# The opening of a recurrence-and-MLP kernel's written order of work, permuted

## The chip, the cores and the metric

The kernel runs on one core of a Trainium2 chip. A core has a matrix engine (TensorE, PE), which loads 64 x 64 weights into its array (PEld) and streams matmuls through it, and three engines for elementwise work: VectorE (DVE), ScalarE (ACT) and GpSimd (POOL). SyncE (SP) only issues DMAs here. Each engine has its own list of instructions and works through it in order; an instruction that has to wait for another engine or for a DMA holds up all that stands behind it on its own engine. Matmuls write to PSUM, from which DVE and ACT read.

The metric is the device time of one execution in microseconds (us). It has to be as low as it can get.

## The reference

Two blocks follow each other. The first is a recurrence over 768 tokens for 4 batches and 8 heads, each with a 40 x 40 state (all in float32):

```python
for t in range(S):
    kt, vt, rt = (k[:, :, t], v[:, :, t], r[:, :, t])
    wt, at, bt = (w[:, :, t], a[:, :, t], b[:, :, t])
    y[:, :, t] = np.einsum('bhd,bhde->bhe', rt, state)
    Sa = np.einsum('bhde,bhe->bhd', state, at)
    state_decay = state * wt[:, :, None, :] - np.einsum('bhd,bhe->bhde', Sa, bt)
    state = state_decay + np.einsum('bhd,bhe->bhde', vt, kt)
```

The second takes `y`, with the 8 heads of a token put side by side to 320 numbers, as 3072 tokens through an MLP with a quick GELU:

```python
h = x @ w_in                               # 320 -> 2048
g = h * (1.0 / (1.0 + np.exp(-1.702 * h)))
return (g @ w_out).astype(np.float32)      # 2048 -> 320
```

## The kernel before, in words

**Tiles and stages.** The sequence is cut into 12 chunks of 64 tokens and the 4 batches into 2 pairs, which gives 24 units; unit i is chunk i // 2 for pair i % 2. Within a unit the 64 steps are not done one by one: the products of the decays are built as exponentials of running sums of their logarithms, the coupling of the 64 tokens through `a` and `b` becomes a triangular 64 x 64 matrix for each head, and this matrix is inverted in five doubling levels. So a unit depends on the unit two places ahead of it (same batches, chunk before) through its state alone. Each unit goes through these steps, by the names of the functions:

- `load_w`, `load`: DMAs of logw and wc (the decay), ak, b, rv, RV (v) and time, all on SP.
- `logarithm` and `decay`: ACT takes the logarithm; PE forms running sums (`by_time` into ps_cum, `by_channel` into ps_cumc); ACT takes exponentials, FT, GT and wch (`exp_of_product`, L565 and L569) and G (`exp_by_time`, L591).
- `prep`: DVE or POOL multiplies ak, b and time by these; PE forms A (`score_A`) and RV (`score_RV`).
- `inverse`: PE forms N (`score_N`), then come five levels. For units 0 to 3 (`plain_level`) a level is 32 + 8 matmuls into ps_level, a copy PT of the pair on ACT (L784) and a transpose EX of the same pair on DVE (L723); the next level needs both. After level 4 come a transpose ES and its spread T (L702, L707), four copies Tc (L797), two half-size products, ps_Q (`off_one`) and ps_T21 (`off_two`), and the finished T on DVE (L830).
- `solve`: from unit 2 on, the state of unit i − 2 is turned and read (ps_zT, ps_rz). The known parts (ps_B0, ps_B1), then ps_X = T times B on PE, M on DVE (L907), then ps_y, whose parts are the new state and the unit's outputs. x, the outputs times FT (`decayed`, L953, on DVE or POOL), goes to DRAM (`part_with`) and comes back transposed as xT (`get_back`).
- `mlp(c)` after every second unit: for q = 0 to 3 ten up matmul groups (`up`, ps_up) and a GELU on ACT, then two down products of eight parts (`down`, ps_down) and a store.

**Weights.** The MLP's weights come as 64-bit words, in 8 weights of 4 DMAs each, and are rebuilt as floats during the opening: `rebased` on ACT (L447), `bounded`, `shifted` and `rounded` on DVE (L451, L455, L459, 128 x 1280 elements each), `joined` on POOL (L463). Weights 0 to 3 are those of up, 4 to 7 those of down; a down product needs all of 4 to 7 part by part.

**The order.** `Plan.add` collects 2700 tasks with their dependencies, numbered in the order of the calls. No scheduler runs at build time: the string `ORDER` is the whole schedule. `Plan.listed` (L89) reads it, and L1046 runs it through:

```python
tasks = plan.listed(ORDER)
for t in tasks:
    t.fn(t)
```

A token such as `209p1` is the number of a task, the engine that does it (p PE, a ACT, d DVE, g POOL, s SP) and, where the task uses PSUM, which of the four pairs of banks it takes. Each engine's instructions come in the order in which their tokens stand. Where two engines read one pair, they do so in turn, in the list's order. A string is allowed if every task stands behind those it depends on, and if the engine is one that the task offers.

SP's DMAs use eight semaphores in turn; in the trace a DMA is issued only once the one eight places ahead of it has landed.

These task numbers come up in the lists:

| task | unit 0 | unit 1 | unit 2 | unit 3 |
|---|---|---|---|---|
| cum, cumc (PE) | 87, 88 | 142, 143 | 264, 265 | 334, 335 |
| A, N (PE) | 98, 103 | 154, 159 | 283, 288 | 353, 358 |
| levels 0 to 4 (PE) | 107, 110, 113, 116, 119 | 163, 166, 169, 172, 175 | 292, 295, 298, 301, 304 | 362, 365, 368, 371, 374 |
| Q, X, y (PE) | 126, 134, 136 | 182, 190, 192 | 311, 326, 328 | 381, 396, 398 |
| x to DRAM, xT back (SP) | 140, 141 | 196, 197 | 332, 333 | 402, 403 |

470 is cum of unit 4; 198 to 207, 209 to 218, 220 to 229 and 231 to 240 are the first MLP's up tasks, 242 to 249 and 253 to 260 its down tasks. Weight 0's DMAs are 15 to 18, and each further weight's are nine numbers on (24 to 27, 33 to 36, up to 78 to 81); the five tasks that rebuild it follow its DMAs.

Of the kernel before, what the change touches and what calls it, by code (L numbers as in the profile page):

```python
# [58 lines left out]
class Plan:  # L59
# [29 lines left out]
    def listed(self, text):  # L89

        assert len(text.split()) == len(self.tasks)
        table, out, done = "exp", [], set()
        for one in text.split():
            e = next(e for e in ENGINES if ENGINES[e] in one)
            n, bank = one.split(ENGINES[e])
            t = self.tasks[int(n)]
            assert e in t.engines and t.after <= done and (e == "SP" or (t.pair is None) == (not bank))
            t.engine, t.bank = e, int(bank or 0)
            if e == "ACT" and t.table:
                t.load, table = t.table != table, t.table  # L100
            done.add(t)
            out.append(t)
        return out
# [4 lines left out]
0s 8s 26s 5s 7s 9s 3a 6s 87p0 88p1 24s 89a1 1s 2s 12s 102a 95d 100p2 90a0 93d 158a 101d2 98p3 96g 10s 94d 17s 97g 16s 99d3  # L108
103p1 4a 11s 132p0 104a1 105d1 142p2 143p3 133a0 106d 130p1 14s 144a3 13s 107p0 15s 18s 151g 108a0 109d0 51s 131a1 110p3 27s
149g 150d 111a3 112d3 159p0 156p1 145a2 161d0 160a0 152g 113p3 345s 92a 162d 25s 153d 114a3 163p2 42s 115d3 34s 19a 274s 264p0  # L110
165d2 265p3 164a2 22d 266a3 166p2 20d 273s 21d 33s 43s 167a2 154p3 168d2 23g 35s 28a 157d1 116p2 155d3 169p1 117a2 118d2 267a0
279d 63s 280g 119p3 277s 171d1 36s 44s 123a3 120d3 343s 125d3 121a 278g 124d3 29d 287a 126p2 170a1 288p0 127a2 30d 172p1 479s
122a3 31d 289a0 128p2 54s 173a1 45s 129d2 32g 62s 174d1 134p3 37a 290d0 175p2 344s 135d3 180a2 146s 178a2 275s 176d2 136p1
179a2 38d 181a2 39d 177a 282g 276s 291d 91s 138a1 182p0 188p3 281d 183a0 186p2 139d 137a1 283p0 187a2 184p1 189a3 40d 140s
292p2 46a 60s 284d0 41g 285p3 185d1 148a 286d3 190p0 293a2 294d2 334p1 335p3 357a 191d0 141s 268g 147s 336a3 315d 192p2 47d
337a1 348d 316p0 194a2 346s 295p3 349d 61s 317a0 195g 347s 358p1 296a3 297d3 360d1 318a0 298p3 271a 361d 319p0 338g 300d3 196s
193a2 320a0 355p2 385d 270s 48d 299a3 362p0 356d2 351g 301p3 363a0 364d0 350g 386p2 197s 302d3 365p0 387a2 269s 352g 359a1
303d3 388a2 323p1 367d0 366a0 321p3 49d 324a1 304p2 322a3 478s 325d1 50g 353p0 309a2 470p3 354d0 209p1 307a2 210p1 310a2 305d2
211p1 308a2 272d 198p0 341a 199p0 72s 212p1 70s 64a 200p0 340s 368p2 52s 342d 339s 69s 201p0 369a2 202p0 370d2 203p0 471a
213p1 65d 214p1 389p2 66d 472a3 483g 204p0 390a2 560s 371p3 67d 306a 53s 215p1 71s 482s 216p1 372a3 217p1 476a 220p2 373d3 68g  # L120
218p1 221p2 477d 219a1 205p0 222p2 206p0 223p2 224p2 78s 559s 207p0 55a 311p3 225p2 79s 312d3 80s 226p2 208a0 58d 313p1 374p3
314d1 227p2 56d 379a3 228p2 229p2 57d 326p0 230a2 59g 393p1 327d0 378a3 391p2 394a1 375d3 231p0 558s 392d2 376a 232p0 233p0
395d1 81s 73a 234p0 480s 381p2 235p0 474s 328p1 475s 382a2 74d 377a3 485d 380a3 236p0 75d 481s 492a 242p2 486d 243p2 82a 76d
484d 77g 383p3 237p0 384d3 244p2 329d1 330d1 488p3 473d 238p0 531d 245p2 487g 246p2 489d3 85d 532p1 708s 239p0 533a1 396p3
331d 534a1 240p0 247p2 397d3 332s 241a0 562s 535p1 83d 490p3 536a1 84d 398p0 706s 572a 491d3 86g 550p1 253p3 399d0 551a 555s
400d0 561s 333s 254p3 401d 255p3 552a1 564d 493p0 402s 556a 567g 570p1 554s 494d0 248p2 705s 563d 566g 249p2 495d0 498d 256p3
571d1 565g 403s 250a2 496a0 251d2 696p1 497g 557d 539p0 252s 537p2 257p3 538a2 704s 540d0 701s 258p3 553d 611d 697a 499d 573p2
259p3 576a2 574d2 784s 710d 700s 260p3 787s 541d0 575d2 404p0 578d 261a3 577g 405p0 579d 698a1 568p2 711g 500p1 406p0 569d2
501a1 407p0 262d3 580p2 702a 502d1 263s 408p0 582d2 409p0 503d 410p0 583d 504a 612p3 411p0 584g 613d3 412p0 614d3 413p0 505p1
709d 414a0 426p3 506d1 427p3 428p3 507d1 429p3 699d 581d2 430p3 615p1 703d 431p3 616a1 785s 585p0 432p3 508d 586a0 433p3 587d0  # L130
434p3 509a 588d 435p3 589d 448p2 436a3 510p1 590p0 511a1 449p2 592d0 591a0 512d1 415p3 513d 416p3 593d 514a 417p3 594g 418p3
515p0 419p3 516a0 517d0 595p1 518d 420p3 596a1 597d1 421p3 598d 422p3 519a 599d 423p3 424p3 520p0 425a3 437p1 521d0 438p1
523d0 522g 439p1 524d0 440p1 525d0 441p1 442p1 526d0 527p3 718p0 528a3 443p1 719d0 929s 444p1 720d0 529p3 445p1 721d0 446p1
530d3 600p0 723d 447a1 542p3 722d 724g 603d0 605a0 619p1 604d0 543d3 450p2 620a1 606d0 544p3 621d1 601d0 602d 617p1 707s 546d3
451p2 618a1 783s 712d 547g 713d 607p0 725p1 608a0 452p2 609p0 453p2 548s 610d0 932s 454p2 727d1 726d1 622p0 728d 545d3 729a
775p1 455p2 623d0 780s 776a 549s 756d 730p3 624p0 456d2 457d2 731d3 458s 459p2 777a1 778g 732d3 786s 788g 781a 779s 626d0
460p2 625d0 627g 733d 795p1 835d 734a 461p2 735p3 791g 462p2 628s 736a3 796d1 737d3 716p0 792g 738d 463p2 782d 739g 1011s
920p1 757p3 925s 464p2 717d0 758a3 629s 759a3 790d 465p2 740p0 789d 466p2 741a0 742d0 921a 797p3 467d2 760p0 1008s 468d2 800a3
923d 652p2 469s 761d0 922a1 653p2 926a 930s 798d3 714p1 799d3 654p2 924s 802d 801g 655p2 934d 803a 656p2 836p0 657p2 715d1
658p2 659p2 837d0 762p3 838d0 927d 660p2 763a3 661p2 764p1 662a2 743d 630p0 744d 928s 631p0 632p0 765d1 804p3 766d1 633p0  # L140
805a3 806d3 634p0 807d 635p0 808a 745p2 636p0 748d2 637p0 749d2 839p1 933g 750d2 638p0 840a1 1009s 751d2 639p0 809p3 746d2
935g 640a0 641p1 810d3 642p1 793p2 747a 811d3 674p0 812d 794d2 813a 752p3 643p1 753a3 814p2 644p1 815a2 816d2 754p3 645p1
755d3 646p1 817d 647p1 818a 767p2 841p3 768d2 648p1 842a3 649p1 819p2 650p1 820a2 821d2 769p3 822d 651a1 823d 675p0 771d3 931s
770d3 772g 824p2 936d 676p0 827a2 828a2 942p1 829a2 677p0 1153s 830a2 937d 945a1 773s 663p3 825d2 664p3 943d1 1156s 826a 665p3
944d1 999p2 947d 946g 666p3 1000a 1004s 980d 940p1 948g 667p3 941d1 668p3 774s 669p3 670p3 831p1 671p3 1001a2 1002d 1003s
832d1 672p3 1005a 1013d 678p0 673a3 1006d 833p2 843p1 679p0 834d2 1007s 844d1 938p2 845d1 680p0 939d2 846p3 681p0 847d3 949p1
# [983 lines left out]
```

## Time and profile before

| what | value |
|---|---|
| time, median of 3 runs | 678.8 us (678.29 to 679.48) |
| profiled execution, its own time | 682.79 us |
| span in the trace, first to last instruction | 681.1 us |
| mean granted TensorE clock | 0.990 |
| DMA bytes moved | 69.73 MB, mean 102 GB/s |

The profiled execution is one of its own and took 4.0 us more than the median of the three timed runs; sums that are made from its rows are made against 682.79, not against 678.8.

How to read it: busy times are summed over an engine's instructions. A digit in the line of slices is the busy share of one fortieth of the span, 17 us, in tenths. PEclk is the granted clock of TensorE on the same scale, where 9 is 90% or more. In tables by stretches, each engine has its busy time, with the number of instructions in brackets, then come the mean granted clock as a share of full speed, the busy share of the DMA engines and the bytes moved in a second. In lists of waits, a row names the waiting engine and line, behind the arrow what released it, then the total in us, how often, and the longest. In the timeline a row has the start and the duration, then engine, line, operation, result and operand; in square brackets stands the engine's idle time just before it, with what ended it.

### The profile page before, as it was taken

Reading aid. Unit: us, or ns where it says so; the run is one execution under the profiler, and the core shown is the slowest. Engines: PE = TensorE matmul, PEld = TensorE weight load, DVE = VectorE, ACT = ScalarE, POOL = GpSimd, SP = SyncE. Lnnn points to the kernel's source line nnn. Section 1 sums busy time; section 2 is a strip of 40 time slices with the busy share of each in tenths; the row PEclk is TensorE's granted clock in tenths of the full one; section 3 lists DMA queues with packets and bytes.
Section 4 is the critical chain, followed back from the end, with each engine's and each line's share of the span. In section 5 each row is a group of like instructions: output and inputs, shape, how many; then the busy total and the mean of one; then the engine's idle time right before and its main releaser. Section 6 shows DMA issues by size and latency. Waiting matters only on the chain.

```text
span 681.1 us, 42181 instructions
## 1 busy us (share of the span) xinstructions
PE 652.0 (96%) x19488; PEld 572.4 (84%) x19488; DVE 445.5 (65%) x906; ACT 330.7 (49%) x688; POOL 176.7 (26%) x204
## 2 busy tenths in 40 slices
PE   5777999999999999999999999999999999999997
PEld 5667888997987788888888898899899799889996
DVE  4687877777867668767776587868556766675001
ACT  4675845544564654664545445455454354252110
POOL 5443444225123123123123211321412421300000
PEclk9788999999999999999999999999999999999999
DMA  7874755205314314432404413513502312200100
GB/s 235 275 244 148 228 158 173 89 14 155 108 50 139 103 45 125 124 108 67 121 23 131 140 34 107 154 33 106 149 29 71 121 51 58 58 13 23 51 12 21
DMA packets 35312, 69.73 MB, mean 102 GB/s; under 512 B 5440, under 2 KB 14656, under 8 KB 35136
## 3 DMA queue, kind: packets, MB, share of 16 engines
q1 hardware_dynamic: 35136, 67.03, 32.8%
q8 instruction: 153, 2.51, 1.6%
q14 instruction: 23, 0.19, 0.1%
HBM read 59.15 MB, written 7.86 MB: 98 GB/s over the span
## 4 chain that ended last, share of the span: by engine, by line
PE 91%; DMA 4%; ACT 1%; DVE 1%; issue 1%; SPq 0%; ACTq 0%; DVEq 0%
PE ps_up L300 31%; PE ps_down L300 30%; PE ps_level L300 9%; PE ps_y L300 5%; PE ps_B L300 4%; PE ps_X L300 2%; PE ps_N L300 2%; PE ps_rz L300 2%; PE ps_RV L300 2%; PE ps_A L300 1%; DMA ak<-in_ak 1%; PE ps_zT L300 1%; PE ps_Q L300 1%; DMA time<-in_time 1%; PE ps_T L300 1%
## 5 line engine op out<-in xcount | busy, mean ns | idle before, releaser
L300 PE MATMUL ps_up<-xT_all,w_sb 64*64 64x256 f32 x3840 | 254.4, 377 | 2.0 <-DMA xT_all<-x_dram 1.1
L300 PE MATMUL ps_down<-w_sb,g 64*64 64x320 f32 x3072 | 240.3, 430 | 1.1 <-issue 0.9
L300 PEld LDWEIGHTS ps_up<-xT_all,w_sb 64*64 64x64 f32 x3840 | 172.9, 133 | 17.7 <-issue 2.5
L300 PEld LDWEIGHTS ps_down<-w_sb,g 64*64 64x64 f32 x3072 | 143.3, 133 | 31.4 <-issue 1.6
L988 ACT ACTIVATE g<-ps_up 128x1024 f32<-128x1024 f32 x48 | 49.1, 1024 | 44.7 <-PE ps_up L300 44.3
L709 POOL TENSOR_TENSOR EX<-ES,quads 128x512 f32<-128x512 f32 x29 | 38.3, 1323 | 115.5 <-DVE ES L702 83.1
L751 ACT COPY W<-ps_level 128x512 f32<-128x512 f32 x56 | 32.7, 585 | 69.1 <-PE ps_level L300 67.4
L300 PEld LDWEIGHTS ps_level<-W,EX 64*64 64x64 f32 x2560 | 59.2, 134 | 5.8 <-DVE T L830 0.2
L300 PE MATMUL ps_level<-W,EX 64*64 64x64 f32 (+1 forms) x2560 | 56.2, 217 | 0.0
L753 DVE TENSOR_TENSOR E<-two,ps_level 128x256 f32<-128x256 f32 x80 | 33.1, 415 | 34.7 <-ACT W L751 30.7
L707 ACT ACTIVATE EX<-ES,quads 128x256 f32<-128x256 f32 x80 | 36.3, 501 | 30.4 <-DVE ES L702 29.9
L619 POOL TENSOR_TENSOR ak<-ak,FT 128x512 f32<-128x512 f32 x16 | 22.0, 1378 | 76.2 <-DMA ak<-in_ak 54.4
L300 PE MATMUL ps_level<-PT,EX 64*64 64x64 f32 (+2 forms) x1280 | 34.9, 244 | 5.7 <-DVE EX L723 4.8
L300 PEld LDWEIGHTS ps_level<-PT,EX 64*64 64x64 f32 x1280 | 32.6, 145 | 8.9 <-DVE EX L723 5.7
L702 DVE STREAM_TRANSPOSE ES<-E 128x256 f32<-128x256 f32 x80 | 35.2, 442 | 4.7 <-DVE E L753 0.5
L300 PE MATMUL ps_y<-M,bh 64*64 64x104 f32 (+1 forms) x768 | 34.8, 247 | 1.3 <-DVE M L907 0.8
L300 PE MATMUL ps_y<-RV,kh 64*64 64x104 f32 (+1 forms) x768 | 34.9, 247 | 0.3 <-DVE EX L723 0.3
L891 ACT COPY B<-ps_B 128x416 f32<-128x416 f32 (+1 forms) x34 | 16.5, 492 | 33.5 <-PE ps_B L300 33.2
L300 PEld LDWEIGHTS ps_y<-RV,kh 64*64 64x64 f32 x768 | 28.9, 133 | 2.0 <-DVE M L907 0.5
L907 DVE TENSOR_TENSOR M<-ps_X,later 128x832 f32<-128x832 f32 (+1 forms) x24 | 23.8, 993 | 9.8 <-PE ps_X L300 9.5
L627 POOL TENSOR_TENSOR kh<-time,G 128x320 f32<-128x320 f32 x18 | 16.2, 902 | 48.4 <-PE ps_y L300 34.4
L300 PEld LDWEIGHTS ps_y<-M,bh 64*64 64x64 f32 x768 | 27.0, 133 | 1.9 <-DVE M L907 1.2
(131 smaller groups left out, 1097.2 us busy)
## 6 DMA issues: line engine op xcount, KB each, us to landing
ak<-in_ak SPq DMA_DIRECT2D x48, 160.0 KB
rv<-in_rv SPq DMA_DIRECT2D x48, 160.0 KB
time<-in_time SPq DMA_DIRECT2D x24, 320.0 KB
xT_all<-x_dram SPq DMA_DIRECT2D x48, 160.0 KB
wc<-in_wc SPq DMA_DIRECT2D x20, 264.0 KB
logw<-in_w SPq DMA_DIRECT2D x24, 160.0 KB
RV<-in_v SPq DMA_DIRECT2D x24, 160.0 KB
b<-in_b SPq DMA_DIRECT2D x48, 80.0 KB
```

The costliest lines, as they stand in the source:

```text
L300: nc.tensor.matmul(o, lhsT, rhs, start=start, stop=True, skip_group_check=True)
L619: plan.add(R, {"DVE": 690.0, "POOL": 1270.0, "sbuf": True}, lambda t: of(t.engine).tensor_mul(ahT(), ahT(), FT_of(i)), reads=T("ak", "FT") ...
L627: plan.add(R + 4, {"POOL": 870.0, "DVE": 490.0, "sbuf": True}, lambda t, n=n, dst=dst: of(t.engine).tensor_mul(dst(i)[:, :, :D], by_head(t ...
L702: plan.add(rank, dve(256), lambda t: nc.vector.transpose(ES(n), source(t)), writes=[key("ES", n, 6)], **reads)
L707: nc.scalar.activation(dst[:, :, h], ES(n), ACT.Copy, scale=quads[:, h, :1])
L709: of(t.engine).tensor_mul(dst, ES(n).unsqueeze(2).to_broadcast([128, 8, 2, 32]), quads.unsqueeze(1).to_broadcast([128, 8, 2, 32]))
L751: plan.add(rank, any2(512), lambda t: copy(t.engine)(tiles_of(W(n + 1)), blocks(psum(t, ""), 64)), writes=[key("W", n + 1, 5)], pair=pair)
L753: plan.add(rank, dve(256), lambda t: nc.vector.tensor_sub(tiles_of(E(n + 1)), every(two32, [128, 2, 4, 32]), blocks(psum(t, ""), 64)[:, :, ...
L891: plan.add(R, any2(4 * wide), lambda t: copy(t.engine)(dst(), some(psum(t, "")[:, :, :208])), writes=[("Bv", i)] if x and c > 0 else T("B" ...
L907: plan.add(R + 1, dve(8 * wide), lambda t: nc.vector.tensor_tensor(M_of(i)[:, :, :wide].rearrange("p (j b) n -> p b j n", b=2), some(psum( ...
L988: plan.add(-45, {"ACT": 1030.0, "table": "gelu"}, lambda t: nc.scalar.activation(g_of(c * NQ + q).rearrange("p m r n -> p r m n"), psum(t, ...
```

## The change

The change has two parts. In `Plan.listed` an SP token may carry a digit, which is stored in a field `window` of the task; no token of the new list has one on SP, and nothing reads the field. And the string `ORDER` is replaced. The new string holds the same 2700 tasks. It differs from the old one in its opening: from PE's 155th task on (of 1080, task 430), ACT's 103rd, DVE's 144th, POOL's 27th and SP's 94th (of 268), each engine's tasks come in the order that they had before. 43 tasks have another engine: DVE has 795 of them (785 before), ACT 427 (433) and POOL 130 (134). The numbers of the PSUM pairs are dealt out anew.

The opening of both lists, to a little beyond the first MLP's first up:

```diff
@@ Plan.listed
             t.engine, t.bank = e, int(bank or 0)
+            if e == "SP":
+                t.window = t.bank
             if e == "ACT" and t.table:
...
 ORDER = """
-0s 8s 26s 5s 7s 9s 3a 6s 87p0 88p1 24s 89a1 1s 2s 12s 102a 95d 100p2 90a0 93d 158a 101d2 98p3 96g 10s 94d 17s 97g 16s 99d3
-103p1 4a 11s 132p0 104a1 105d1 142p2 143p3 133a0 106d 130p1 14s 144a3 13s 107p0 15s 18s 151g 108a0 109d0 51s 131a1 110p3 27s
-149g 150d 111a3 112d3 159p0 156p1 145a2 161d0 160a0 152g 113p3 345s 92a 162d 25s 153d 114a3 163p2 42s 115d3 34s 19a 274s 264p0
-165d2 265p3 164a2 22d 266a3 166p2 20d 273s 21d 33s 43s 167a2 154p3 168d2 23g 35s 28a 157d1 116p2 155d3 169p1 117a2 118d2 267a0
-279d 63s 280g 119p3 277s 171d1 36s 44s 123a3 120d3 343s 125d3 121a 278g 124d3 29d 287a 126p2 170a1 288p0 127a2 30d 172p1 479s
-122a3 31d 289a0 128p2 54s 173a1 45s 129d2 32g 62s 174d1 134p3 37a 290d0 175p2 344s 135d3 180a2 146s 178a2 275s 176d2 136p1
-179a2 38d 181a2 39d 177a 282g 276s 291d 91s 138a1 182p0 188p3 281d 183a0 186p2 139d 137a1 283p0 187a2 184p1 189a3 40d 140s
-292p2 46a 60s 284d0 41g 285p3 185d1 148a 286d3 190p0 293a2 294d2 334p1 335p3 357a 191d0 141s 268g 147s 336a3 315d 192p2 47d
-337a1 348d 316p0 194a2 346s 295p3 349d 61s 317a0 195g 347s 358p1 296a3 297d3 360d1 318a0 298p3 271a 361d 319p0 338g 300d3 196s
-193a2 320a0 355p2 385d 270s 48d 299a3 362p0 356d2 351g 301p3 363a0 364d0 350g 386p2 197s 302d3 365p0 387a2 269s 352g 359a1
-303d3 388a2 323p1 367d0 366a0 321p3 49d 324a1 304p2 322a3 478s 325d1 50g 353p0 309a2 470p3 354d0 209p1 307a2 210p1 310a2 305d2
-211p1 308a2 272d 198p0 341a 199p0 72s 212p1 70s 64a 200p0 340s 368p2 52s 342d 339s 69s 201p0 369a2 202p0 370d2 203p0 471a
...
+0s 2s 7s 8s 5s 9s 3a 6s 87p0 88p1 1s 26s 100p2 13s 89a1 146s 15s 90a0 93d 95d 101d2 98p3 12s 96d 10s 94d 4a 92a 33s 99d3 102a
+14s 97d 130p1 103p0 132p2 11s 105d0 143p3 106d 133a2 131a1 16s 142p2 104d0 17s 107p1 144a3 24s 51s 18s 108a1 149d 145a2 109d1
+158a 110p0 153g 150d 112d0 159p3 111d0 156p2 161d3 113p1 345s 157d2 277s 151d 25s 27s 114a1 162d 35s 274s 152d 19a 163p0 115d1
+52s 265p2 164a0 22d 116p1 160a3 273s 165d0 20d 166p3 43s 21d 264p0 266a2 118d1 23g 168d3 28a 117d1 154p2 155d2 119p1 267a0
+167a3 279d 63s 34s 29d 45s 169p0 123a1 60s 278g 36s 120d1 344s 171d0 121a 270s 268g 30d 91s 280g 287a 126p2 170a0 288p3 127d2
+125a1 289d3 172p2 343s 290d3 122a1 124a1 31d 44s 173a2 128p0 32g 129d0 174d2 134p3 37a 275s 175p1 135d3 178a1 38d 136p0 148a
+179a1 39d 181a1 291d 188p2 137a0 282g 276s 186p3 176d1 42s 138a0 180d1 281g 177a 283p0 139d 189a2 182p1 292p2 183a1 40d 140s
+187a3 147s 357a 184p1 284d0 41g 285p3 293a2 185d1 334p0 46a 286d3 190p1 141s 294d2 335p3 269s 191d1 295p2 336a3 47d 192p1
+337a0 315d 296a2 349d 355p3 346s 194a1 316p0 348d 347s 193a1 195g 338d 297d2 317a0 358p1 318a0 298p2 360d1 361d 359a1 319p0
+196s 299a2 385d 362p1 352g 341a 300d2 350g 364d1 301p2 320a0 356d3 197s 363a1 386p0 303d2 323p3 340s 387a0 388a0 49d 321p1
+302a2 365p0 324d3 478s 325d3 62s 304p2 48d 366a0 61s 198p3 339s 322a1 199p3 50g 367d0 200p3 271a 310d2 368p1 305d2 307d2 209p0
+369d1 210p0 308a2 211p0 309a2 69s 212p0 351d 70s 201p3 370d1 71s 202p3 479s 272d 389p2 470p1 203p3 390a2 213p0 306d 471a 214p0
+342d 353p2 204p3 472a1 485g 474s 205p3 72s 476a 371p1 354d2 53s 482s 64a 480s 206p3 477d 215p0 473g 54s 216p0 492a 220p2 221p2
...
```

## The prediction

> **What bounds the kernel now.** I read the page's busy times and slices first. TensorE (PE) is busy 96% of the span, and only the first slices and the last have idle time.
>
> ```profile
> PE 652.0 (96%) x19488; PEld 572.4 (84%) x19488; DVE 445.5 (65%) x906; ACT 330.7 (49%) x688; POOL 176.7 (26%) x204
> PE   5777999999999999999999999999999999999997
> PEclk9788999999999999999999999999999999999999
> ```
>
> The change permutes the opening alone and PE's list is the same from its 155th task on, so its worth is PE's idle time in the first 70 us (four slices of 17 us). A table by stretches shows where (columns: stretch, its length, busy us of PE, weight load, DVE, ACT and POOL, clock, DMA share, GB/s).
>
> ```profile
> 0.00:26.00 26.00, 16.31 (x436) 15.02 (x440) 12.39 (x21) 11.46 (x32) 13.27 (x45) 0.87 0.79 243
> 26.00:48.00 22.00, 14.98 (x596) 13.15 (x592) 18.26 (x33) 16.59 (x44) 9.74 (x5) 0.92 0.88 280
> 48.00:58.00 10.00, 7.23 (x312) 6.37 (x304) 7.15 (x12) 7.22 (x19) 5.00 (x7) 1.00 0.65 199
> 58.00:69.00 11.00, 9.82 (x400) 9.34 (x396) 8.26 (x12) 5.99 (x14) 4.89 (x4) 0.84 0.31 86
> 69.00:95.00 26.00, 25.32 (x673) 22.05 (x666) 21.76 (x28) 21.39 (x44) 9.37 (x5) 1.00 0.73 230
> ```
>
> Between 26 and 69 PE idles 43.0 − 32.0 = 11.0 us; after 69, where the MLP's first up matmul starts (69.0), hardly at all. So the question is at what time PE reaches that up with its other work done, and whether it can run on. The waits up to 70 us name what it waits for.
>
> ```profile
> DVE EX L723 <- ACT PT L784: 11.7, 8, 3.2
> PE ps_level L300 <- DVE EX L723: 4.8, 5, 1.7
> PE ps_Q L300 <- ACT T L707: 3.2, 2, 2.0
> ```
>
> These are the inversion of units 0 and 1: level on PE, copy PT on ACT, transpose EX on DVE, next level. The transpose reads the same PSUM pair as the copy and starts when the copy ends. The timeline shows that list order, too, costs time.
>
> ```profile
> 25.41 1.50 DVE L723 STREAM_TRANSPOSE EX<-ps_level 128x512 f32<-128x512 f32 x2 [1.63 <-ACT PT L784]
> ...
> 29.18 0.69 PE L300 MATMUL ps_A<-ak 40*64 40x64 f32 x32 [0.28 <-ACT wch L569]
> ...
> 30.63 0.89 PE L300 MATMUL ps_level<-PT,EX 64*64 64x96 f32 x32 [0.76 <-DVE EX L723]
> ```
>
> The two transposes at 25.41 belong to units 0 (level 2) and 1 (level 0). Unit 0's was done at 26.13, but its level 3 began at 30.63, because PE's list has cum and cumc of unit 2, unit 1's level 1 and unit 1's A (waiting for ACT's exponentials) before it.
>
> Last, the clock, in windows of 3.41 us.
>
> ```profile
> 15.72:19.14 3.42, 1.73 (x63) 1.31 (x61) 0.72 (x1) 1.78 (x8) 1.86 (x2) 1.00 0.86 297
> 19.14:22.55 3.41, 2.82 (x90) 2.45 (x86) 1.99 (x3) 1.14 (x2) 1.50 (x2) 0.50 0.90 316
> 32.79:36.20 3.41, 0.92 (x40) 0.67 (x40) 3.24 (x8) 1.44 (x6) 2.44 (x2) 1.00 0.93 287
> 36.20:39.62 3.42, 3.34 (x100) 3.35 (x104) 2.43 (x4) 2.18 (x8) 0.84 (x1) 0.50 0.80 288
> 56.68:60.10 3.42, 1.49 (x64) 1.35 (x68) 3.08 (x6) 2.12 (x5) 0.41 (x1) 1.00 0.59 196
> 60.10:63.51 3.41, 3.41 (x108) 3.38 (x100) 2.03 (x2) 1.48 (x3) 3.28 (x3) 0.50 0.62 178
> ```
>
> Half clock follows a window with at most 1.73 us of PE work, never one with 2.13 or more. A half-clock window costs up to 1.7 us of PE work.
>
> **The change, part by part.** It removes and adds no instruction: 2700 tasks before and after. The added line stores a field that nothing reads. What moves is order, the engine of 43 tasks, and pair numbers. I follow the two dependency chains through the new lists with durations from before's rows, and DMA landings from before's, shifted by the bytes ahead of each at 243 to 280 GB/s.
>
> *SP.* logw of unit 1 moves behind logw of unit 0 and a piece of weight 0 goes ahead of unit 1's rv and ak: I get ak(0) 7.8 us (6.72 before), logw(1) 10.3 (11.49), ak(1) 17.1 (15.83), b(1) 19.5 (18.14). With eight DMAs in the air an issue follows a landing (5.79 after 5.78), so these slips add. Weight 0's last piece slips from 21.41 to about 25.0, and the last of weight 3 to about 40.3 from 37.69; late weights hold up ACT, which rebases them in list order. Unit 1's level 0 ends up at 24.5 against 24.11: nothing gained up to there.
>
> *PE and ACT, 26 to 48.* Unit 0's level 3 is now listed ahead of unit 2's sums: from 30.63 to 26.5. Level 4 goes from 33.41 only to 31.95, because DVE and ACT take other work between. Unit 0's Q goes from 36.28 to 35.4, its X from 40.56 to 39.05, its state from 42.72 to 40.85. Unit 1's level 2 gets later (31.56 to 33.45: unit 2's exponentials and weight 1 stand ahead of its copy on ACT), its level 3 earlier (37.61 to 36.65), and its Q not at all (45.53 to 45.55: ACT, in order, waits for that late weight piece). Gain here: 1.7 us on unit 0, 0 on unit 1.
>
> *26 to 40, clock.* The new list leaves PE some 1.55 us of work in 29.4 to 32.8, under 1.73, so I take half clock from 32.8 to 39.6. It costs unit 0 0.9 us (X at 39.95); unit 1 waits for the weight anyway. Ends: 0 and 0.9; I take 0.9, which changes nothing in the sum below, since unit 1 ends it.
>
> *48 to 69.* Unit 1's X comes at 48.3 (49.54), its y ends at 52.3 (53.96). Unit 2's levels now stand before unit 1's work, not behind it: its level 2 at 54.2 (57.76), its rz at 55.3 (58.69). From about 49.7 PE has no stall over 0.5 us, where before it idled 2.8 us in 48 to 58 and 1.2 in 58 to 69, and ran at half clock from 60.10 to 63.51; with PE full from 50 on that window goes. PE reaches the first up at 62.5 instead of 69.01: 6.5 us earlier. Before, its list has A of unit 3 (0.70) and cum of unit 4 (0.45) ahead of it, now behind: 6.5 − 1.15 = **5.35 us**. The up's input xT of unit 1 lands at about 60.6 (62.45), 1.9 us before it is needed.
>
> *DVE and POOL.* DVE gets 10 tasks more (18.4 us in 26.5 to 45.8, 95%; before 18.26 of 22, 83%). A weight's tensor_scalar takes 0.82 us alone and 1.53 at 44.43, beside a POOL operation: +0.7. Of 12 in before's first 69 us two met one. In the new lists I find two more, in the stretch where unit 1 has no slack (1.4 us); ends: none (0) and all twelve (8.4). I take 1.4, by the one or two met in before. 5.35 − 1.4 = **4.0 us**.
>
> *After 69.* PE now reaches the first down at 90.0 (93.53). Its weight, joined by POOL, comes at 89.0 (89.56). It fits by 1.0. Then the lists agree and PE, busy 97%, keeps the lead.
>
> The profiled execution took 682.79 (span 681.1), 4.0 above the median of 678.8, so it becomes 678.8, and the median 678.8 − 4.0 = **674.8**. Differences of up to 0.2% (1.4 us) can hardly be told from no change.
>
> **The clock, by trace and by rule.** Before 19.14, 36.20 and 60.10 the clock halved after windows in which PE was busy 1.73, 0.92 and 1.49 us of 3.41, its longest gaps being 1.25 to 1.95 us. The Trainium skill's "TensorE: Matmul & The Clock Gate" ("Part 1: The HAM clock gate" and "Why this matters for your kernels") lets the half clock come back only after at least one idle window, and asks to avoid gaps over some 3 us. By that rule nothing in the changed kernel would go cold and the 0.9 us above would be saved; the trace disagrees three times, so I keep its pattern.
>
> **The rivals.**
> - *More half clock.* The new list moves idle time about, and two more windows may fall to 1.73 or less, in 39 to 50. Each costs up to 1.7 us: 674.8 + 3.4 = 678.2. For it: the pattern, and PE's work in 39 to 50 is thin. Against: unit 1 then waits on DMA and ACT, not PE.
> - *The lead is given back at the first down.* PE comes at 90.0, the weight at 89.0, a spare of 1.0 in a chain of four DMAs, ACT, DVE and POOL. If four DMAs and DVE slip by 4.5, PE waits 3.5: 678.3. Against: DMA share falls to 0.31 at 58 to 69, so that late loads have room.
> - *Slower: DVE is the bound.* At 95% in 26 to 46, all that meets POOL falls on the chain. If all twelve weight operations meet it, 12 × 0.7 = 8.4, and 5.35 − 8.4 = −3.05: 678.8 + 3.05 = 681.9. It decides from eight of twelve (5.6). For it: in 48 to 69, too, DVE gets more. Against: two of twelve before.
> - *Nothing of it reaches the ups*, since xT of unit 1 lands late: that needs 1.9 us beyond my landing; half of the gain goes at 4.6. Inside the first rival's price.
>
> **How the numbers follow.** My forecast 0.56 (own range 672.3 to 677.4: the early landings ±0.9 us, half the POOL meetings either way 0.7, clock 0.9); more half clock, or xT late, 0.18; first down 0.07; DVE bound 0.19. Faster by over 0.2% (below 677.4): 0.56 + 0.06 of the second and third = 0.62. Same: 0.15, the most of those. Slower: 0.19 and 0.04 of the second, 0.23. The range runs from 671.5 (5.35 gained, no meetings, one cold window fewer by 1.7, rounded in) to 681.5, short of the full slower case.
>
> **What would show it.** Level 3 of unit 0 at about 26.5, unit 1's Q at about 45.5, unit 1's y ending near 52.3, first up near 62.5, full clock from 40 on, no idle before the first down at 90. Wrong: first up after 66, weight tensor_scalars of 1.5 us by the handful, half clock in 40 to 60, or PE waiting for w_sb near 90.

## The result and the profile after

The new order is slower. In the first measurement it took 686.39 us (685.27 to 687.62, 4 runs) against 679.14 us before (678.29 to 680.0, 4 runs): a ratio of 1.0107, 95% interval 1.0085 to 1.0129. Measured again later it came to 1.0111 (1.0075 to 1.0146). The forecast was 674.8, faster by 0.6%.

The profiled execution of after took 685.27 us (span 683.6), the fastest of its four, while that of before took 682.79 and was slow for its kernel. So the two profiles lie 2.5 us apart where the medians lie 7.3 apart. The lines of after's page that answer to those shown of before, busy times and PE's slices:

```profile
PE 650.0 (95%) x19488; PEld 555.8 (81%) x19488; DVE 449.6 (66%) x918; ACT 328.0 (48%) x680; POOL 168.9 (25%) x200
PE   5677899899999999999999999999999999999996
```

And the table by stretches, with the same columns as before's:

```profile
0.00:26.00 26.00, 14.22 (x428) 12.65 (x432) 15.77 (x28) 10.48 (x29) 7.78 (x41) 1.00 0.83 257
26.00:48.00 22.00, 15.35 (x587) 13.46 (x581) 19.90 (x33) 14.78 (x41) 10.54 (x8) 0.92 0.85 269
48.00:58.00 10.00, 8.09 (x367) 7.12 (x359) 6.55 (x12) 7.34 (x20) 4.17 (x5) 1.00 0.40 115
58.00:69.00 11.00, 8.20 (x336) 7.37 (x335) 7.40 (x13) 6.62 (x13) 4.53 (x4) 1.00 0.50 146
69.00:95.00 26.00, 24.29 (x671) 22.38 (x669) 18.46 (x33) 16.63 (x32) 7.93 (x5) 1.00 0.52 170
```

The stretch that was to become dense, 48 to 69, has PE busy for 16.3 of 21 us; before had 17.1, with half clock in 3.4 of them. The first up starts at 67.7 instead of 69.0, where the forecast had 62.5. What PE waits for between 45 and 75 us is hardly an engine any more (0.9 of 7.6 us). The longest waits of after:

```profile
PE ps_level L302 <- issue: 2.5, 3, 1.2
PE ps_up L302 <- issue: 1.6, 1, 1.6
PE ps_X L302 <- issue: 0.9, 1, 0.9
PE ps_y L302 <- issue: 0.7, 1, 0.7
PE ps_Q L302 <- issue: 0.7, 1, 0.7
PE ps_level L302 <- DVE EX L725: 0.4, 1, 0.4
```

"issue" is time in which PE waited for nothing that the profile shows. The timeline of PE shows these waits in the middle of a task, where all operands have long been there:

```profile
59.14 0.56 PE L302 MATMUL ps_level<-PT,EX 64*64 64x96 f32 x16 [1.16 <-issue]
...
62.95 0.24 PE L302 MATMUL ps_level<-PT,EX 64*64 64x96 f32 x1 [0.43 <-issue]
...
66.56 0.40 PE L302 MATMUL ps_level<-PT,EX 64*64 64x96 f32 x9 [0.86 <-issue]
```

If one counts all of PE's instructions from the start (weight loads, matmuls, and the 302 semaphore instructions and drains between them, which the page does not count as busy), these waits stand ahead of numbers 1985, 2241, 2497, 2753, 3009, 3265 and 3521: every 256th instruction. The seven are 6.4 us together; of the rows above only the last is none of them. The page has a queue of its own for code, here after's:

```profile
q8 instruction: 153, 2.51, 1.5%
```

153 packets of 16 KB for 39,278 PE instructions: 256 instructions to a packet. In this stretch of the trace a packet of this queue starts 1.1 to 1.5 us after PE has passed one of these instructions (3.4 after the 3265th, beside a burst of loads), takes 0.9 to 1.4 us, and PE goes on 1.3 to 1.7 us after its end. So a block of code is there some 3.7 us after the one ahead of it was begun.

This gives a better ruler than the start of the first up, before which the two lists have done different work: the times at which PE passes the same number of instructions. From task 155 on both lists are the same, so at the 7617th (near 145 us) both have done the same work.

| us, from the traces | 1985th | 3521st | 7617th | 1985th to 3521st | 3521st to 7617th |
|---|---|---|---|---|---|
| before, first profile | 47.2 | 71.1 | 144.8 | 24.0 | 73.7 |
| after, first profile | 47.5 | 72.2 | 148.3 | 24.7 | 76.1 |

The middle stretch, where the gain was to come from, takes no less with the new list, and most of the 3.5 us that after has lost by the 7617th (2.5) comes behind it. There the second MLP waits for its input xT (after):

```profile
122.34 0.61 PE L302 MATMUL ps_up<-xT_all,w_sb 64*64 64x256 f32 x2 [1.43 <-DMA logw<-in_w]
123.47 2.18 PE L302 MATMUL ps_up<-xT_all,w_sb 64*64 64x256 f32 x27 [0.52 <-DMA xT_all<-x_dram]
```

(The first row names logw, a load whose landing came at about that time; what task 404 needs is xT of unit 3, whose two halves landed at 122.10 and 123.34, in before at 116.64 and 117.08 for an up at 121.46.) The clock then halves from 124.6 to 128.0. xT was late for two reasons. x of unit 3 took DVE 3.38 us beside three operations on POOL, where before had 1.43; and SP issued the fetch (403) at 117.50 instead of 113.18. After:

```profile
109.70 3.38 DVE L955 TENSOR_TENSOR x<-zr,FT 128x128 f32<-128x128 f32 x4
```

Before:

```profile
108.58 1.43 DVE L953 TENSOR_TENSOR x<-zr,FT 128x128 f32<-128x128 f32 x4
```

Executions of one and the same kernel differ by some 10 us here (before alone, 33 runs: 677.7 to 688.0), so that ratios have intervals of 0.2 to 0.4% to either side and each experiment is read in its trace first. A trace, too, is one execution: a difference of 1 or 2 us between two traces can be chance.

### The profile page after: what moved, and what is told of

Same layout as the page of the kernel before. It is cut to its first block, busy times and chain, and to the rows that moved or that the text cites. A ratio compares the mean times of both kernels' runs of the same rounds, so it can differ in the third digit from the quotient of the medians.

```text
span 683.6 us, 42180 instructions
## 1 busy us (share of the span) xinstructions
PE 650.0 (95%) x19488; PEld 555.8 (81%) x19488; DVE 449.6 (66%) x918; ACT 328.0 (48%) x680; POOL 168.9 (25%) x200
## 4 chain that ended last, share of the span: by engine, by line
PE 89%; DMA 4%; DVE 3%; issue 2%; SPq 1%; ACT 1%; ACTq 0%; DVEq 0%
PE ps_up L302 31%; PE ps_down L302 29%; PE ps_level L302 9%; PE ps_y L302 5%; PE ps_B L302 4%; PE ps_X L302 3%; PE ps_rz L302 1%; PE ps_RV L302 1%; DMA xT_all<-x_dram 1%; PE ps_N L302 1%; PE ps_A L302 1%; DMA b<-in_b 1%; PE ps_zT L302 1%; PE ps_Q L302 1%; DMA ak<-in_ak 1%
## 5 line engine op out<-in xcount | busy, mean ns | idle before, releaser
L302 PEld LDWEIGHTS ps_up<-xT_all,w_sb 64*64 64x64 f32 x3840 | 170.2, 134 | 22.5 <-issue 4.7
L302 PEld LDWEIGHTS ps_down<-w_sb,g 64*64 64x64 f32 x3072 | 129.7, 133 | 41.5 <-ACT zr L871 0.4
L753 ACT COPY W<-ps_level 128x512 f32<-128x512 f32 x56 | 32.8, 585 | 67.3 <-PE ps_level L302 65.6
L709 ACT ACTIVATE EX<-ES,quads 128x256 f32<-128x256 f32 x84 | 38.1, 501 | 31.3 <-DVE ES L704 30.7
L302 PE MATMUL ps_level<-PT,EX 64*64 64x64 f32 (+2 forms) x1280 | 33.4, 236 | 10.2 <-DVE EX L725 3.4
L302 PEld LDWEIGHTS ps_level<-PT,EX 64*64 64x64 f32 x1280 | 31.0, 139 | 13.7 <-issue 5.0
L909 DVE TENSOR_TENSOR M<-ps_X,later 128x832 f32<-128x832 f32 (+1 forms) x24 | 23.9, 995 | 9.5 <-PE ps_X L302 9.3
L302 PEld LDWEIGHTS ps_B<-RV,A 64*64 64x64 f32 x768 | 25.0, 137 | 4.9 <-ACT PT L406 1.3
L302 PE MATMUL ps_B<-RV,A 64*64 64x104 f32 (+1 forms) x768 | 27.9, 253 | 1.1 <-ACT PT L406 1.1
```

The costliest lines, as they stand in the source:

```text
L302: nc.tensor.matmul(o, lhsT, rhs, start=start, stop=True, skip_group_check=True)
L709: nc.scalar.activation(dst[:, :, h], ES(n), ACT.Copy, scale=quads[:, h, :1])
L753: plan.add(rank, any2(512), lambda t: copy(t.engine)(tiles_of(W(n + 1)), blocks(psum(t, ""), 64)), writes=[key("W", n + 1, 5)], pair=pair)
L909: plan.add(R + 1, dve(8 * wide), lambda t: nc.vector.tensor_tensor(M_of(i)[:, :, :wide].rearrange("p (j b) n -> p b j n", b=2), some(psum( ...
```

## The experiments

The theories at the start: L, the loss lies behind the first up, in the late xT; O, it lies in the opening. Then C, PE's code sets the time of the dense stretch; D, what PE waits for are DVE and ACT. Last S, the order of the DMAs makes after slower (S1: the first of them alone); E, the order of the compute tasks does.

### Before once more

No edit.

> The kernel before, once more, to have its profile beside the others of this chip. Both theories: within 0.2% of before (679 us). What it tells apart: the first profiled execution of before took 682.8 us, 4 us above its median. If the half clock windows of that trace (3 of 3.4 us in the first 70) are what made it slow, this profile has fewer of them and is near 679; if profiling itself costs that, it is near 683 again.

Measured: 682.45 us median (12 runs), ratio 1.0002 (0.997 to 1.0035). The profiled execution took 684.76. It has no half-clock window in its first 682 us and is still 2 us slower than the first one, which had 13.65 us of them. So the half clock is not what made the first one slow. In the opening, the waits of PE between 45 and 75 us in this second profile of before say why full clock brings nothing:

```profile
PE ps_zT L300 <- issue: 1.5, 1, 1.5
PE ps_level L300 <- issue: 1.4, 1, 1.4
PE ps_level L300 <- DVE EX L723: 1.2, 1, 1.2
PE ps_B L300 <- issue: 1.1, 1, 1.1
PE ps_cum L300 <- issue: 0.9, 1, 0.9
PE ps_rz L300 <- issue: 0.6, 1, 0.6
PE ps_A L300 <- issue: 0.4, 1, 0.4
```

That is 6.0 us for code, ahead of the 1985th, 2241st, 2497th, 2753rd, 3009th and 3265th instruction; the first profile had 1.6 from the 1985th to the 3521st, and none ahead of the 3009th, where its half clock (60.10 to 63.51) had made PE slower than its code. At full clock the code is slower than PE, and the same instructions take 25.4 us instead of 24.0. The two executions alone could be chance, but the traces of all lists below say the same: with half clock in that stretch it took 23.5 to 25.2 us (seven traces), without it 23.9 to 25.4 (five). Before was at this wall, too, and its first profile showed little of it. What the 2 us are stays open: between 280 and 495 us the second execution falls some 3 us back, in many small steps.

### The two halves, exchanged

Opening from one list up to the first up, all that is left from the other: first after's 249 tokens, then before's order; then before's 253 tokens (up to 353p0, four tokens short of its first up), then after's order.

```diff
 ORDER = """
-0s 8s 26s 5s 7s 9s 3a 6s 87p0 88p1 24s 89a1 1s 2s
+0s 2s 7s 8s 5s 9s 3a 6s 87p0 88p1 1s 26s 100p2 13s
...
+325d3 62s 304p2 48d 366a0 61s
 479s 54s 271a 351g 367d0 322a1 50g 353p0 309a2 470p3
...
```

> After's list up to its first up matmul (249 tokens over all engines), then every task left in before's order. Theory L (the loss lies behind the opening: the second MLP's first up waits for xT of unit 3, which after fetches 5.7 us later): the loss is gone, 678 to 680 us. Theory O (the opening itself makes it slower, on PE's code or on DVE): 684 to 687, as after.

```diff
 ORDER = """
 0s 8s 26s 5s 7s 9s 3a 6s 87p0 88p1 24s 89a1 1s 2s
...
 324a1 304p2 322a3 478s 325d1 50g
+52s 341a 340s 198p3 339s 199p3 200p3 310d2 368p1 305d2
...
```

> Before's list up to its first up matmul (253 tokens), then every task left in after's order. Theory L: the loss is there without after's opening, 683 to 687 us, with PE waiting for xT of unit 3 near 121. Theory O: 678 to 680.

Measured: after's opening with before's rest 684.01 us, 1.0040 (1.0010 to 1.0069); before's opening with after's rest 683.46 us, 1.0024 (0.9992 to 1.0056). Neither theory holds alone: after's opening loses by itself, and the loss by after's rest alone is not clear of noise in the time. The traces put a part in each half (table below): from the 3521st to the 7617th, before's rest takes 72.4 us behind after's opening, too, and after's rest 74.3 behind before's, with a wait of 1.17 us until 120.60 ahead of the second MLP's first up.

### The fetch of xT first

```diff
-402s 539p1 564d 554s 493p0 567g 540a1 257p2 705s 496a0 541d1 556a 704s 494d0 249p3 566g 495d0 403s
+402s 403s 539p1 564d 554s 493p0 567g 540a1 257p2 705s 496a0 541d1 556a 704s 494d0 249p3 566g 495d0
```

> After with one token moved: the fetch of xT of unit 3 (403, on SP) stands right behind the store that it needs (402), ahead of wc of a later unit, b and ak. Theory L: xT lands at about 119 instead of 122.1, PE no longer waits the 1.9 us at 121 to 123 and the half-clock window behind it (1.7 us) goes: 3.6 us less than after, about 682.8. Theory O: as after, 686.4.

Measured: 685.95 us, 1.0068 (1.0034 to 1.0101). The wait for xT is gone from the trace, but the stretch behind the 3521st takes 76.0 us as before the edit: the profile now has a wait for code of 1.8 us ahead of the 5313th instruction, at 106.4 us. After, run again, has that one, too (1.5 us at 107.2). So the late xT is one of several things that cost there, and its price could not be told from the noise: the interval overlaps that of after.

### After once more, and the two halves by engine

> The kernel after, once more, on the chip of the others. Theory C: its trace has a wait at every 256th PE instruction between 45 and 72 us (5 to 7 us in all), as the second profile of before had (6.0), so that six blocks of code take 23 to 25.5 us in both; time 684 to 687. Rival D: waits elsewhere, as DVE and POOL happen to meet; six blocks within 22 us in one of the traces.

Measured: no edit; 689.24 us where before had 681.69: 1.0111 (1.0075 to 1.0146). The waits stand at the 256th instructions again, the 1985th to the 3521st take 23.9 us, as C has it. But the 1985th comes only at 51.3.

Then after's compute lists with before's list of DMAs (all 268 SP tokens; the opening of SP's list is shown), and the reverse:

```diff
-0s 2s 7s 8s 5s 9s 6s 1s 26s 13s 146s 15s 12s 10s
+0s 8s 26s 5s 7s 9s 6s 24s 1s 2s 12s 10s 17s 16s
...
```

> After's lists on PE, ACT, DVE and POOL with before's list of DMAs on SP. Theory S (the order of the DMAs makes after slower: late weights and b in the opening, late xT of unit 3 at 121): 680 to 682 us, and PE's 1985th instruction near 46.5 us. Theory E (the order and engines of the compute tasks make it): 684 to 687, and the 1985th instruction near 48.5.

> Before's lists on PE, ACT, DVE and POOL with after's list of DMAs on SP. Theory S: 683 to 687 us, 1985th PE instruction near 48.5 us, PE waiting near 121 for xT of unit 3. Theory E: 680 to 682, 1985th instruction near 46.5.

Measured: 699.78 us, 1.0269 (1.0244 to 1.0293), and 690.40 us, 1.0125 (1.0096 to 1.0154). Both theories fall. The DMAs' order and the compute order belong together: after's compute with before's DMAs is slower than both kernels, before's compute with after's DMAs as slow as after. In the first, PE waits 5.6 us for ACT from 67.5 on and 5.0 us for rv of a later unit from 104.8 on, though before's DMAs bring PE's 705th instruction at 20.6 us (22.2 and 24.8 in the two profiles of after).

### The first DMAs alone

SP's first 19 tokens from before in after; the same with before's rest; and the first 20 from after in before.

```diff
-0s 2s 7s 8s 5s 9s 6s 1s 26s 13s 146s 15s 12s 10s 33s 14s 11s 16s 17s 24s 51s 18s ...
+0s 8s 26s 5s 7s 9s 6s 24s 1s 2s 12s 10s 17s 16s 11s 14s 13s 15s 18s 146s 33s 51s ...
```

> After with its first DMAs in before's order: SP's first 19 are before's (ak and b of units 0 and 1 earlier, pieces of weights 0 and 1 instead of wc of unit 3 and a piece of weight 2), the others follow in after's order; nothing else moves. Theory S1 (the landings of ak and b set the first 25 us; what is late there stays late, since the code of PE leaves no room to catch up between 47 and 72): PE's 705th instruction at 20.5 to 22.5 us instead of 22.2 to 24.8, its 1985th near 46.5 instead of 47.5 to 51.3, and 2 to 3 us less than after: 684 to 686 where before has 681. Theory E (the order of the compute tasks in 26 to 47 is what costs): the 705th earlier, but the 1985th still at 48 to 51, and the time within 1 us of after's 688.

> The same opening (after's compute tasks up to the first up, before's first 19 DMAs), and before's order for all that follows the first up. S1: no loss left in either half, and the compute order's own gain of 1 to 2 us can show: 679 to 681.5 where before has 681. E: as the run with after's opening and before's rest, 683 to 685.

> Before with SP's first 20 DMAs in after's order, the others in before's; nothing else moves. S1: PE's 705th instruction at 24 to 26 us (22.3 in before), the 1985th 2 us or more later than before's 46.6, and 2 to 4 us slower than before: 683 to 685. E: within 1 us of before.

Measured: 687.35 us, 1.0089 (1.0049 to 1.0129); 684.18 us, 1.0060 (1.0037 to 1.0083); 683.10 us, 1.0026 (0.9993 to 1.0059). In the first, the 705th instruction comes at 23.0, and the 1985th at 52.0 all the same: E, the compute order between 26 and 47, comes out right here, and in the second, too, where the 1985th comes at 49.6. The third speaks for S1: 705th at 24.3 and 1985th at 50.6, so the late first loads alone cost before 2 and 4 us in the trace. But this was the slowest of its twelve executions (690.4), and the time over all of them is unclear. So the loss is there without the late first loads, which may cost something of their own. That the order of the compute tasks makes it alone is not shown, since the DMAs behind the 19th stood in after's order in both runs.

The other traces by the same ruler (us). The two whose lists of DMAs were exchanged are left out; there the middle took 28.9, with the 5.6 us of waiting for ACT in it, and 24.5.

| list | 1985th | 3521st | 7617th | 1985th to 3521st | 3521st to 7617th |
|---|---|---|---|---|---|
| before, second profile | 46.1 | 71.4 | 143.8 | 25.4 | 72.4 |
| before's opening, after's rest | 46.5 | 70.0 | 144.3 | 23.5 | 74.3 |
| before, first DMAs of after | 50.6 | 75.9 | 147.9 | 25.2 | 72.0 |
| after, second profile | 51.3 | 75.2 | 151.1 | 23.9 | 75.9 |
| after, xT first | 48.8 | 72.8 | 148.8 | 24.1 | 76.0 |
| after's opening, before's rest | 49.8 | 73.8 | 146.1 | 24.0 | 72.4 |
| after, first DMAs of before | 52.0 | 76.2 | 152.5 | 24.2 | 76.3 |
| the same, before's rest | 49.6 | 74.7 | 146.8 | 25.1 | 72.1 |
| after, one copy on ACT (below) | 49.9 | 74.2 | 148.7 | 24.3 | 74.4 |

Three things stand out. The 1536 instructions in the middle take 23.5 to 25.4 us with any of these lists, although PE's waits for code in them add up to anything from 1.5 to 6.4 us: what PE does not lose to code, it loses to engines or to half clock. Behind them before's rest takes 72.0 to 73.7 us and after's, behind after's opening, 74.4 to 76.3: some 3 us more. And after's opening reaches the 1985th at 49.3 on average (47.5 to 51.3, its four profiles with its own DMAs), before's at 46.6 (three): 2.7 us later, not earlier. The four runs below that add matmuls to before have its order up to there as well, and pass it at 47.3, 47.4, 49.3 and 47.2; with them before's mean is 47.3 and the difference 2.1.

### The code by itself

Behind the end of before, matmuls that depend on nothing:

```diff
     for t in tasks:
         t.fn(t)
+    def fed(cols, count, rhs):
+        for k in range(count):
+            r, h = QUARTERS[k % 4]
+            mm(feed[HALF[h], r, :cols], w_out_sb[CHANNELS[r], :64], rhs[CHANNELS[r], :cols], True)
+    for cols, count in ((32, 1024), (104, 1024), (256, 384), (64, 1024)):
+        fed(cols, count, w_out_sb)
...
+    for n in range(4):
+        for m, (of, src) in enumerate(((time_of, time_d), (time_of, time_d), (ak_of, ak_d), ...
+            nc.sync.dma_start(of(NU - 2 + m % 2), src[2 * n + m % 2])
+    fed(64, 1024, w_out_sb)
```

> Before, and behind its end 4576 more matmuls that depend on nothing and whose results nobody reads: 1024 of 32 columns, 1024 of 104, 384 of 256, 1024 of 64, then 24 matmuls and 1024 of 64 columns beside 24 loads. Theory C (PE's code comes in blocks of 256 instructions and a block takes some 3.7 us from its request to its use): with 32 and 64 columns every 256 PE instructions (128 weight loads and 128 matmuls) take 3.6 to 3.9 us, with one wait of about 1 us at each 256th; with 104 columns 3.6 to 3.9 with a small wait; with 256 columns 13.7 us and no wait; beside loads up to 5 us. Rival D (the waits in the opening come from dependencies on DVE and ACT alone): 32 and 64 columns run through at 2.7 us per 128 matmuls, no waits, as nothing is waited for.

Measured: 1034.47 us with its tail, one run. Each matmul of the program is two matmuls and two weight loads in the trace, so that 64 of them make a block. The clock was half for nearly all of this tail. With 32 columns and quiet DMAs the first 128 matmuls, still at full clock, took 1.85 us; at half clock, where 128 take 3.42 by their own time, eight blocks took 29.1 us, 3.64 each, the single ones 3.5 to 4.0. With 104 and 256 columns nothing waits, at this half clock. Beside the loads (DMA engines 91% busy) a block takes 5.7 to 6.2 us; the timeline of PE:

```profile
972.95 3.69 PE L300 MATMUL ps_feed<-w_sb 40*64 40x64 f32 x128 [2.52 <-issue]
979.16 3.69 PE L300 MATMUL ps_feed<-w_sb 40*64 40x64 f32 x128 [2.52 <-issue]
```

128 matmuls, a wait with nothing to wait for, 128 matmuls: D has no place for this. In the same stretch the code's packet starts 3.2 to 3.9 us after PE has begun a block, where with quiet DMAs it starts 1.0 to 1.5 us after. The full-clock rate of C could not be read here, as the clock was half; the run with three blocks more has it.

### More code in the dense stretch

Narrow matmuls into unread columns, behind levels 2 and 3 of unit 2 and 0 and 1 of unit 3 in before; then 32 each behind levels 2 and 3 of unit 3, among the first ups; then 48 in each of the first four.

```diff
+            count = {(2, 2): 16, (2, 3): 16, (3, 0): 16, (3, 1): 16}.get((i, n), 0)
+            def and_more(t):
+                go(t)
+                for k in range(count):
+                    r, q = QUARTERS[k % 4]
+                    mm(psum(t, "")[HALF[q], r, 448:480], ident[HALF[r]], ident[HALF[r], :32], False)
+
...
+            plan.add(rank, pe((4, wide), (1, 128)), and_more, reads=[key("EX", n, 5), ("PV", turn(i, n, 5))], uses=T("PT"),
```

> Before with 64 narrow matmuls more (weights and operand the identity, 32 columns, into columns of the PSUM pair that nobody reads), 16 each in levels 2 and 3 of unit 2 and 0 and 1 of unit 3, which lie at 55 to 66 us. They are 256 PE instructions, one block of code; run for themselves such matmuls took 1.85 us at full clock. Theory C: a whole block more has to come in, so PE's 256 x 15 instructions from the 1985th to the 3777th take 27 to 29 us, where the 1536 to the 3521st took 23.5 to 25.4 in all runs so far. Theory D (waits on DVE and ACT; PE's own time): the narrow matmuls fill those waits or add 1.85 us at most: 24 to 26.

> The same 64 narrow matmuls, but 32 each in levels 2 and 3 of unit 3, which stand among the first ups at 72 to 78 us, where a block of code lasts PE longer than 4 us. Theory C: no wait is added, only their own 1.85 us: from the 3521st to the 5057th PE instruction some 25.3 to 26 us, against 23.5 to 24.8 for the same work without them (to the 4801st). Theory D: the same 1.85 us. It is the control to the run above.

Measured, one run each: 680.29 us with the block in the dense stretch and 682.42 with it among the ups, where before in the same session had 678.71 (674.59 to 684.10, 13 runs): both times lie within before's own. With one block more, the 1985th to the 3777th took 26.4 us, between the two theories. From the start of unit 1's y to the first up it took 20.7 us; the two profiles of before and the run with more code behind the first up have 17.4, 18.5 and 17.6 there. So it cost 2.3 to 3.3 us: more than its own 1.85, less than the 3.7 of a block, and not clear of the differences between runs. The control failed as one: the 3521st to the 5057th took 26.7 us and not 25.3 to 26, and had a wait of 1.3 us ahead of the 3777th. That 128 instructions put into one level make a dense block there, too, would explain it, but is not shown.

> As the run with 64 narrow matmuls more among the levels at 55 to 66 us, but with 192 (48 in each of the same four levels): 768 PE instructions, three blocks of code, 5.55 us of PE's own time at full clock. One block had come out between the theories (from unit 1's y to the first up 20.7 us, against 17.4 to 18.5 without). Theory C: each block costs 3.6 to 4 us: from unit 1's y to the first up 28 to 30.5 us, with waits at the 256th instructions. Theory D: at most their own 5.55 us: 23 to 24.

Measured: 691.47 us where before had 681.01, one run each, and 27.05 us from y to the first up (51.95 to 79.00), 8.6 to 9.6 more than without, where their own time is 5.55: 2.9 to 3.2 us for each block. This is C's side, though less than C's 28 to 30.5. The timeline of PE has the waits at the 256th instructions, the longer ones inside the added matmuls, which depend on nothing that is late:

```profile
65.95 0.67 PE L300 MATMUL ps_level<-ident 64*64 64x32 f32 x33 [2.02 <-issue]
...
69.68 0.79 PE L300 MATMUL ps_level<-ident 64*64 64x32 f32 x41 [1.37 <-issue]
...
73.13 1.37 PE L300 MATMUL ps_level<-ident 64*64 64x32 f32 x81 [1.25 <-issue]
```

Here the rate of the code can be read at full clock, too. From 65.95 on three blocks follow each other with a wait for code at each end, DMA engines 2% busy: they take 3.73, 3.45 and 4.01 us, of which PE is busy for 2.2 to 2.5.

### One wait of the new opening taken away

In the new list the copy of level 3 of unit 0 (task 117) went from ACT to DVE, behind two weight operations and two transposes; in its traces PE waits 1.8 us for it ahead of level 4.

```diff
-264p0 266a2 118d1 23g 168d3 28a 117d1 154p2 155d2 119p1
+264p0 266a2 117a1 118d1 23g 168d3 28a 154p2 155d2 119p1
```

> After with one of the 43 engine choices undone: the copy of level 3 of unit 0 (task 117), which after does on DVE behind two weight operations and two transposes, is on ACT again, ahead of weight 1's rebasing. In six traces of after's opening PE waited 1.75 to 1.79 us for it ahead of level 4. Theory E (this wait is what makes the opening late): the wait goes to 0.5 or less, level 4 starts 1.5 us earlier after its level 3, and the 1985th PE instruction comes 1.5 us earlier than after's mean of 49. Theory C: the wait goes, but the block of code at PE's 1217th instruction, which lies in that same level 4, comes no earlier (3.7 to 6 us behind the 961st), so that the wait for it grows from 0.3 to 2.6 by about as much, and the 1985th instruction and the time stay (1.009 to 1.011 of before).

Measured: 684.12 us, 1.0073 (1.0037 to 1.0109), not to be told from after. The traces tell. Level 4 of unit 0 in the second profile of after:

```profile
33.93 0.43 PE L302 MATMUL ps_level<-PT,EX 64*64 64x32 f32 x16 [1.79 <-DVE PT L786]
36.15 0.65 PE L302 MATMUL ps_level<-PT,EX 64*64 64x32 f32 x16 [1.79 <-issue]
```

And with the copy on ACT:

```profile
32.22 0.43 PE L298 MATMUL ps_level<-PT,EX 64*64 64x32 f32 x16 [0.41 <-DVE EX L721]
34.74 0.55 PE L298 MATMUL ps_level<-PT,EX 64*64 64x32 f32 x13 [2.09 <-issue]
```

The wait for DVE went from 1.79 to 0.41, and half-way through the same level stands the 1217th instruction, whose code comes 6.2 us after the 961st was passed, beside full DMAs (5.8 and 7.1 us in the two profiles of after). Its second half starts at 34.74, and the 1985th instruction comes at 49.9. In both profiles of before the 961st to the 1217th took 4.0 us, with no wait for code; in two of the runs that add matmuls to before further on, it took 4.6 and 5.4, with waits for code of 0.35 and 1.15. Full DMA engines are not the whole difference: they were 92 and 93% busy there in the two profiles of before, 95 and 91% in those of after. The packet of code starts 0.7 and 1.4 us after the 961st in before, 3.3 and 4.7 in after (3.5 with the copy on ACT). Why it starts later with the new list stays open.

## Why the prediction was wrong

**Milestones up to 40 us: right.** In the first profile level 3 of unit 0 started at 26.59 (forecast 26.5), level 4 at 31.76 (31.95), Q at 35.60 (35.4), X at 40.41 (39.95); level 2 of unit 1 at 33.42 (33.45), its Q at 46.38 (45.55). Landings, too: ak(1) 17.77 (17.1), weight 0's last piece 24.34 (25.0). But before's own landings had been read some 1.1 us too early: its ak(1) landed at 17.05 (POOL took it up at 17.27) and not 15.83, its last piece of weight 0 at 22.46 and not 21.41. Other executions of the same list run up to 4 us later from 16 us on, as the landings and the code do.

**"From about 49.7 PE has no stall over 0.5 us": wrong, and this is the step that failed.** It was to give the 5.35 us. PE has seven waits of 0.4 to 1.6 us there, all for code, 6.4 us together; y of unit 1 ended at 55.85 and not 52.3, the first up came at 67.7 and not 62.5. I had taken PE's idle time for slack that another order can use. Two rows of before's own waits up to 70 us showed what sets it, and I passed over them, since a wait for nothing seemed no wait that an order could meet:

```profile
PE ps_rz L300 <- issue: 0.8, 1, 0.8
PE ps_zT L300 <- issue: 0.6, 1, 0.6
```

An estimate from the three blocks at full clock in the run with three blocks more (3.5 to 4.0 us, 3.73 on average): the six blocks from the 1985th to the 3521st need some 22 us in any order. Before took 24.0 and 25.4 for them, so there was no room for the 5.35.

**The measure was wrong, too.** I followed unit 1's chain and took what PE did beside it as free. Behind it stands a wall that counts instructions: the end of the dense stretch goes by when the 1985th is passed, and after passes it 2.1 to 2.7 us later. The forecast saw the idle place (only 1.55 us of PE work in 29.4 to 32.8, the weight that holds up ACT) and priced it at nothing, because unit 1 waited anyway. With the 3 us behind the 3521st (below) this is 5 to 6 of the 7.3 us by which the medians differ; the rest is within the spread of executions and is not located. So the runs show why the gain did not come; why the new order is even slower they show only in part: where it falls back, and which waits stand there.

**The half clock.** Forecast from 32.8 to 39.6 and none near 60: in the first profile 32.5 to 35.9, in the second 20.9 to 24.3 and 34.5 to 48.2. The price of 1.7 us for a window has no place where code is the limit: seven traces with one from the 1985th to the 3521st were no slower there than five without. The pattern itself was misread, too. In before, the half-clock window from 22.55 follows one with 2.82 us of PE work, itself at half clock; and in the first profile of after, windows with 1.43 and 1.13 us of work (5.41 to 12.24) had full clock behind them. The rule of the Trainium skill ("TensorE: Matmul & The Clock Gate") that a whole idle window is needed for the half clock does not hold in the new traces either: PE was busy for 1.35 us ahead of 32.5 and for 1.74 ahead of 124.6.

**DVE beside POOL: the mechanism was right, the place was not.** The 1.4 us were put on weight operations in 26 to 46. What showed was x of unit 3 at 109.7, 3.38 us, beyond the window that I followed.

**"Then the lists agree and PE keeps the lead": wrong.** Up to PE's 155th task they do not agree, and after's order there takes some 3 us more than before's behind the same opening (74.4 to 76.3 against 72.1 and 72.4): a late xT, a wait for code near 106, a half-clock window, one or two of them in each execution. Weight 4 came at 95.6, 6.6 later than forecast, but PE came to the first down only at 95.8, so that it did not wait for it.

**The slower rival** had the right sign for a wrong reason. DVE was said to be the bound from 26 on; in 45 to 75 PE waits 0.4 us for it. Its one wait that counted, 1.8 us for the copy, turned into a wait for code when it was taken away.

## What to carry to other kernels

Before one prices idle time on TensorE as slack, one should count its instructions: where a block of 256 of them lasts less than some 4 us (here, small matmuls at full rate), waits that end by "issue" at every 256th are a wall, and a wait that is removed ahead of it can come back there, as the copy's did. Two orders are best compared at the same count of work done on the busy engine, not at a milestone before which they did different things. And an order found on an estimate is worth what the estimate covers: here the milestones by hand knew nothing of the code, and an order of DMAs could not be judged apart from the order of compute that it feeds.

## What the runs showed of the hardware

- PE's code comes in blocks of 256 instructions through a DMA queue of its own (153 packets of 16 KB for 39,278). The packet of the next block starts only after a block is begun, and its code is usable 3.5 to 4.0 us after that with quiet DMAs (at full clock in the run with three blocks more), 5.7 to 6.2 us beside loads that keep the DMA engines 91% busy. The Trainium skill ("Runtime: NRT & Kernel Launch", "Instruction fetch mechanics") has the blocks, and says that the cost of crossing one is mostly hidden. With 64 x 64 float32 matmuls of up to 104 columns it is not: waits of 0.2 to 2.6 us, 6.0 us in the first 75 of before's second profile and 6.7 in after's first. Beside loads it was not hidden behind a block with 320 columns either: 1.5 us ahead of the 5313th in after's second profile, where the packet started 3.8 us after the 5057th.
- Half clock does not follow idleness alone: behind the end of before, PE ran at clock 0.50 for 355 us with matmuls that depend on nothing, 40 x 64 weights and 32 to 256 columns, back to back but for the waits for code.
- The four DVE operations of one x (128 x 128 each) took 3.38 us beside POOL operations on other tiles, 1.43 where POOL was busy in the first 0.7 and the last 0.2 us of them, and 0.88 with POOL idle (x of unit 0 in before).
